# Transposing four token tiles on TensorE between query chunks, and loading eight tiles from SP's queue

## The chip, the cores and the metric

The kernel runs on one core of a Trainium2 chip. The metric is the device time of one execution in microseconds (us). The engines are named as in the profile: PE (TensorE: matmuls, with its weight loads as PEld), DVE (VectorE), ACT (ScalarE), POOL (GpSimd) and SP (SyncE, which here only issues DMAs). Each engine works through its own instructions in order. DMAs are issued in order by the engine in whose program they stand; they then share the core's 16 DMA engines.

## The reference

`x` has 2048 tokens of 512 values. It is normalised, and the result `xn` goes two ways: attention `A` with 32 heads of 128 against given keys and values (2048 each), and a mixer with an MLP, `B`, whose `silu` gates the attention's output.

```
xn = layernorm(x)                                    # 2048 x 512
A:  q = xn @ wq  (32 heads x 128);  p = softmax(q k^T / sqrt(128));  s = (p v) @ wo
B:  h = gelu(layernorm(xn) @ w1);  four column groups of h shifted by +1, -1, +2, -2 tokens
    x1 = xn + shifted(h) @ w2;  b = x1 + gelu(layernorm(x1) @ w3) @ w4      # F = 1792
out = x + s * silu(b)
```

Inputs and output are bf16.

## The kernel before

Tokens are worked in 16 tiles of 128 (`t`), and in four groups of 512 columns (`qt`). `xall[:, t, :]` holds normalised tile `t` with tokens on the partitions. Matmuls that contract over the 512 features need it transposed: `xnT`, four blocks of 128 features with all tokens as columns. The second layer norm of `B` is of an already normalised tile, so `m1` takes `xnT` as it is.

The order on every engine is written out by hand: each instruction is pinned in program order. The work up to the attention goes as follows.

- `load_x(t, eng)` (L153) loads a tile into `xin`, one of ten buffers of tag `ta`. Tiles 0 to 3 are loaded from SP and ACT, 4 to 7 from SP, 8 to 15 from GpSimd.
- `ln1_stats(t)` takes mean and variance on DVE (L172, L173) and the inverse root on POOL (`rsqrt`, L167, L168); `ln1_norm(t)` writes `xall` on DVE (L177) and frees `xin`.
- `tr_pe(t)` transposes a tile by four matmuls against the identity into one of the two PSUM buffers of `psO` and copies it to `xnT` on ACT (L191); `tr_dma(t)` does it with one transposing DMA on SP's queue (L194). Before, tiles 0 to 3 take the first way, all others the second.
- `m1(c0, w)` is the first product of `B` (PE, and gelu on ACT, L205); `m2(t)` the second, from the shifted columns, into `psO`; `x1(t, ps)` adds it to `xall` on DVE (L217).
- `q_ahead(u)` is one query chunk: four matmuls of 512 columns into a `psX` buffer, and a copy to `qT` on ACT (L269). Sixteen of them, one head and one `qt` each, are made ahead of the attention. Chunks 0 to 3 need `xnT` of tiles 0 to 3 alone.
- The seven loads of `w3` (L423) and that of `w2` (L384) stand on SP's queue; `ln2(t)` transposes the second normalised tiles by DMA on the same queue (L225); `m3` and `m4` are the MLP.

A DMA on SP or ACT also waits for the landing of the one eight DMAs earlier in their common program order, whose semaphore it takes over. All matmuls have line L106, a helper, so they are told apart by their tiles: `ps_q` is a query chunk, `ps_s<-xnT,w_sb` is `m1`, `ps_o<-w_sb,hT` is `m2`, and `ps_o<-ident,xall` is a transposition.

Behind this start lie the MLP (to about 129 us) and the attention with the output projection, in which scores, exponentials and the products with `v` run in slots (to the end). PE's order around the change is: transpositions and `m1` of tiles 0 to 3, query chunks 0 to 3, `m2(0)` and `m2(1)`, `m1(512, 512)` (tiles 4 to 7), chunks 4 to 7, `m2(2)` and `m2(3)`, `m1(1024, 512)` (tiles 8 to 11), and so on.

Of the kernel before, what the change touches and what calls it, by code (L numbers as in the profile page):

```python
# [17 lines left out]
def kernel(  # L18
# [15 lines left out]
    nc = tc.nc  # L34
    P = nc.NUM_PARTITIONS
# [12 lines left out]
    FC = F // P  # L48
    EPS = 1e-5
    SCALE = float(Dh) ** -0.5  # L50
    HG = 4
# [10 lines left out]
    pin = tc.keep_in_program_order  # L62
# [40 lines left out]
    w3_v = B_w3.rearrange("(dc p) f -> p dc f", p=P)  # L103

    def mm(out, lhsT, rhs, start, stop):
        pin(nc.tensor.matmul(out=out, lhsT=lhsT, rhs=rhs, start=start, stop=stop))  # L106
# [7 lines left out]
        out=ident[:], in0=diag[:], scalar1=0.0, scalar2=None, op0=ALU.is_equal))  # L114
# [36 lines left out]
    def load_x(t, eng):  # L151
        xin[t] = tokp.tile([P, D], BF16, tag="ta", bufs=10, name="xin")
        pin(eng.dma_start(out=xin[t][:], in_=xsrc[t]))  # L153
# [5 lines left out]
    w3_sb = [pL.tile([P, DC, 2 * P], BF16, name=f"w3_sb{i}") for i in range(FC // 2)]  # L159
# [21 lines left out]
    def ln1_stats(t):  # L181
        stats(xin[t][:], mv1, rs1, t)

    def ln1_norm(t):
        norm_to(xall[:, t, :], xin.pop(t)[:], mv1, rs1, t)

    def tr_pe(t):
        tp = psO.tile([P, DC, P], FP32, tag="ps_o", name="ps_o")
        for dc in range(DC):
            mm(tp[:, dc, :], xall[:, t, dc * P:(dc + 1) * P], ident[:], True, True)  # L190
        pin(nc.scalar.activation(out=xnT[:, :, t * P:(t + 1) * P], in_=tp[:], func=ACT.Identity))  # L191

    def tr_dma(t):
        pin(nc.sync.dma_start_transpose(out=xnT[:, :, t * P:(t + 1) * P], in_=xall[:, t, :]))  # L194

    def m1(c0, w):
        for jp in range(DC // 2):
            b = BASE_J[2 * jp]
            ps = psS.tile([P, 2, 512], FP32, name="ps_s")
            for j in range(2):  # L200
                jc = 2 * jp + j
                for dc in range(DC):
                    mm(ps[:, j, 0:w], w1_sb[:, dc, jc * P:(jc + 1) * P],
                       xnT[:, dc, c0:c0 + w], dc == 0, dc == DC - 1)
            pin(nc.scalar.activation(  # L205
                out=hT[:, 2 * jp:2 * jp + 2, b + c0:b + c0 + w], in_=ps[:, :, 0:w],
                func=ACT.Gelu_apprx_tanh))

    def m2(t):
        ps = psO.tile([P, D], FP32, tag="ps_o", name="ps_o")  # L210
        for jc in range(DC):
            c0 = BASE_J[jc] + t * P - SHIFT[jc]
            mm(ps[:], hT[:, jc, c0:c0 + P], w2_sb[:, jc, :], jc == 0, jc == DC - 1)
        return ps
# [41 lines left out]
    def q_mm(u, dcs, tag="xa"):  # L256
        g, qt, hh = units[u]
        if dcs[0] == 0:
            st[u] = dict(psq=psX.tile([P, 512], FP32, tag=tag, name="ps_q"))
        for dc in dcs:  # L260
            mm(st[u]["psq"][:], wqs[g * HG + hh][:, dc, :],
               xnT[:, dc, qt * 512:(qt + 1) * 512], dc == 0, dc == DC - 1)

    def q_copy(u, eng=None):
        qT = qtp.tile([P, 512], BF16, name="qT")
        if eng is None:
            pin(nc.vector.tensor_copy(out=qT[:], in_=st[u].pop("psq")[:]))  # L267
        else:
            pin(nc.scalar.activation(out=qT[:], in_=st[u].pop("psq")[:], func=ACT.Identity))  # L269
        st[u]["qT"] = qT  # L270
# [133 lines left out]
    ln1_norm(3)  # L404
    tr_pe(3)
    m1(256, 256)
    for t in range(8, 12):
        load_x(t, nc.gpsimd)

    def ln1_block(ts):  # L410
        ln1_stats(ts[0])
        for a, b in zip(ts, ts[1:]):
            ln1_stats(b)
            ln1_norm(a)
            tr_dma(a)
        ln1_norm(ts[-1])
        tr_dma(ts[-1])

    ln1_block(range(4, 8))
    for t in range(12, 16):  # L420
        load_x(t, nc.gpsimd)
    for i in range(FC // 2):
        pin(nc.sync.dma_start(out=w3_sb[i][:], in_=w3_v[:, :, i * 2 * P:(i + 1) * 2 * P]))  # L423
    def q_ahead(u):
        q_mm(u, range(DC), ("xa", "xm")[u % 2])
        q_copy(u, nc.scalar)

    for u in range(HG):
        q_ahead(u)
    pend = [(t, m2(t)) for t in range(2)]  # L430
    ln1_block(range(8, 12))
    m1(512, 512)
    for t, ps in pend:
        x1(t, ps)
    for u in range(HG, 2 * HG):
        q_ahead(u)
    pend = [(t, m2(t)) for t in range(2, 4)]
    ln1_block(range(12, 16))
    m1(1024, 512)
    for t, ps in pend:  # L440
        x1(t, ps)
# [92 lines left out]
    for n in range(NS + 3 * SPU):  # L534
        u, p = divmod(n, SPU)
# [25 lines left out]
        if p == 6 and wo_todo:  # L561
            gg, t = wo_todo.popleft()
# [13 lines left out]
    while wo_todo:  # L576
        gg, t = wo_todo.popleft()
# [36 lines left out]
```

## Time and profile before

| what | value |
|---|---|
| median of 3 runs | 1289.25 us (1289.19 to 1290.49) |
| profiled execution | 1289.44 us, span 1287.6 us |
| mean granted clock of TensorE | 0.991 |
| PE busy | 1257.4 us, 98% of the span |
| ACT busy | 1054.8 us, 82% |
| DVE busy | 942.5 us, 73% |
| POOL busy | 47.5 us, 4% |
| DMA | 91.57 MB, mean 71 GB/s |

The span runs from the first to the last instruction of the core; the time of the execution holds the little that lies around it. A row of instructions gives their start, their duration, the engine, the line, the operation, what is written from what, and their count; in brackets stands how long the engine was idle before and what ended that wait. A matmul's duration holds its way through the array, so matmuls in a row overlap, and what each costs is read from the distance of starts. "Granted clock" is the share of full speed that PE's clock was allowed; `PEclk` 1.00 is full.

### The profile page before, as it was taken

What the parts mean: (1) busy time and instruction counts of PE and PEld (TensorE: products, weight loads), DVE (VectorE), ACT (ScalarE), POOL (GpSimd) and SP (SyncE); (2) the same over time, 40 slices, a digit from 0 to 9 for tenths busy, and PEclk for the clock granted to TensorE, in tenths of its full rate; (3) what the DMA queues carried; (4) which work ended last, traced back from release to release, by engine and by line L of the source; (5) the groups of instructions that cost most, each with busy time, mean ns of one, the idle gap of its engine ahead of it and who ended that gap; (6) DMA issues with size and microseconds to landing.
All of it is one profiled execution on the core that took longest, in us unless ns stands there. A gap on an engine that the chain in (4) does not pass through costs nothing.

```text
span 1287.6 us, 16764 instructions
## 1 busy us (share of the span) xinstructions
PE 1257.4 (98%) x6128; PEld 609.6 (47%) x6252; DVE 942.5 (73%) x1316; ACT 1054.8 (82%) x1101; POOL 47.5 (4%) x115
## 2 busy tenths in 40 slices
PE   7999999999999999999999999999999999999995
PEld 3444444444444444444444444444444444444442
DVE  6721467777777777777777777777777777778886
ACT  4344779998888888888888888888888888888882
POOL 5320000000000000000000000000000000000000
PEclk9999999999999999999999999999999999999997
DMA  9293122443144522452145423451244323442211
GB/s 209 45 172 74 21 46 50 82 91 67 41 74 77 97 34 51 90 96 46 48 83 77 79 42 59 90 95 33 55 91 78 62 51 72 85 82 43 65 43 49
DMA packets 170771, 91.57 MB, mean 71 GB/s; under 512 B 124928, under 2 KB 153088, under 8 KB 170688
## 3 DMA queue, kind: packets, MB, share of 16 engines
q1 hardware_dynamic: 166464, 84.72, 34.3%
q0 software_dynamic: 1824, 4.98, 1.7%
q8 instruction: 49, 0.80, 0.3%
q10 hardware_dynamic: 2400, 0.79, 0.2%
q14 instruction: 34, 0.28, 0.1%
HBM read 67.63 MB, written 2.36 MB: 54 GB/s over the span
## 4 chain that ended last, share of the span: by engine, by line
PE 89%; DVE 6%; DMA 2%; ACT 1%; issue 1%; POOL 0%; another core or an unknown queue 0%; SPq 0%; DVEq 0%; ACTq 0%
PE ps_s L106 36%; PE ps_o L106 35%; PE ps_wo L106 8%; PE ps_q L106 7%; DVE acc L294 2%; PE ps_m L106 2%; PE ps_sum L106 1%; ACT pT L283 1%; DVE sacc L365 1%; DVE xall L369 1%; DVE acc L299 1%; DMA kT<-in_A_k_cache_dram 1%; DVE qT L267 0%; DVE xl L371 0%; DMA xnT<-xall 0%
## 5 line engine op out<-in xcount | busy, mean ns | idle before, releaser
L283 ACT ACTIVATE pT<-ps_s 128x1024 bf16<-128x1024 f32 x1024 | 993.1, 1026 | 135.3 <-PE ps_s L106 130.4
L106 PE MATMUL ps_o<-pT,vb 128*128 128x512 bf16 x2030 | 605.0, 379 | 3.3
L106 PE MATMUL ps_s<-qT,kT 128*128 128x512 bf16 x1986 | 596.8, 380 | 3.9 <-ACT pT L283 1.2
L294 DVE TENSOR_TENSOR acc<-acc,pT 128x2048 bf16<-128x2048 bf16 x256 | 312.3, 1220 | 72.3 <-ACT pT L283 71.2
L106 PEld LDWEIGHTS <-kT 128*128 128x128 bf16 x2048 | 222.0, 113 | 203.0 <-issue 6.1
L106 PEld LDWEIGHTS <-vb 128*128 128x128 bf16 x2048 | 199.9, 98 | 225.7
L289 DVE TENSOR_TENSOR acc<-pT 128x2048 bf16<-128x2048 bf16 x128 | 156.8, 1225 | 51.2 <-ACT pT L283 51.2
L106 PE MATMUL ps_wo<-wo_h,oT 128*128 128x512 bf16 x509 | 154.5, 387 | 6.2 <-DVE sacc L365 3.1
L365 DVE TENSOR_TENSOR sacc<-ps_wo,sacc 128x512 f32<-128x512 f32 x112 | 77.4, 691 | 89.5 <-PE ps_wo L106 88.7
L106 PE MATMUL ps_q<-xnT,wq_h 128*128 128x512 bf16 x481 | 141.6, 379 | 0.2
L299 DVE TENSOR_TENSOR acc<-acc 128x1024 bf16<-128x1024 bf16 x128 | 88.5, 691 | 4.4
L333 DVE TENSOR_TENSOR oT<-ps_o,rb 128x512 bf16<-128x512 f32 x128 | 87.3, 682 | 2.6 <-DMA rb<-dr 2.6
L106 PEld LDWEIGHTS <-oT 128*128 128x128 bf16 x512 | 50.4, 99 | 70.2 <-issue 7.6
L106 PEld LDWEIGHTS <-wq_h 128*128 128x128 bf16 x512 | 50.0, 98 | 60.4 <-issue 0.3
L267 DVE CAST qT<-ps_q 128x512 bf16<-128x512 f32 x112 | 76.3, 682 | 0.0
L300 DVE TENSOR_TENSOR acc<-acc 128x512 bf16<-128x512 bf16 x128 | 54.4, 425 | 4.4
L106 PEld LDWEIGHTS <-acc 128*128 128x128 bf16 x512 | 37.6, 116 | 34.2 <-issue 4.0
L355 POOL DMA_DIRECT2D xl<-in_A_x_dram x16 | 8.7, 543 | 1137.4 <-DMA out_dram<-xl 1014.3
L106 PE MATMUL ps_s<-xn2T,w_sb 128*128 128x512 bf16 x220 | 48.6, 379 | 0.2
L106 PEld LDWEIGHTS <-w_sb 128*128 128x128 bf16 x304 | 30.0, 99 | 39.1 <-issue 7.7
L234 ACT ACTIVATE h2T<-ps_s 128x1024 bf16<-128x1024 f32 x28 | 28.7, 1024 | 24.0 <-PE ps_s L106 23.3
L319 DVE RECIPROCAL rc<-ps_sum 128x4 f32<-128x4 f32 x128 | 23.2, 181 | 21.3 <-PE ps_sum L106 7.2
(45 smaller groups left out, 332.2 us busy)
## 6 DMA issues: line engine op xcount, KB each, us to landing
rb<-dr SPq DMA_DIRECT2D x128, 256.0 KB, 4.3
vb<-in_A_v_cache_dram SPq DMA_DIRECT2D x64, 256.0 KB, 4.4
wo_h<-in_A_wo_dram SPq DMA_DIRECT2D x32, 128.0 KB, 4.2
wq_h<-in_A_wq_dram SPq DMA_DIRECT2D x28, 128.0 KB, 4.5
w_sb<-in_B_w_dram SPq DMA_DIRECT2D x9, 256.0 KB, 5.4
kT<-in_A_k_cache_dram SPq DMA_TRANSPOSE x128, 4.4
xl<-in_A_x_dram POOLq DMA_DIRECT2D x16, 128.0 KB, 2.3
dr<-rc SPq DMA_DIRECT2D x128, 2.0 KB, 1.4
```

What stands on the lines that cost most here:

```text
L106: pin(nc.tensor.matmul(out=out, lhsT=lhsT, rhs=rhs, start=start, stop=stop))
L234: pin(nc.scalar.activation(out=h2[c, f][:], in_=ps[:], func=ACT.Gelu_apprx_tanh))
L267: pin(nc.vector.tensor_copy(out=qT[:], in_=st[u].pop("psq")[:]))
L283: pin(nc.scalar.activation(out=s["pT"][-1][:, jj:jj + 2, :], in_=sps[:], func=ACT.Exp, scale=SCALE))
L289: pin(nc.vector.tensor_tensor(out=s["acc"][:], in0=s["pT"][0][:], in1=s["pT"][1][:], op=ALU.add))
L294: pin(nc.vector.tensor_tensor(out=a[:], in0=a[:], in1=st[u]["pT"][i][:], op=ALU.add))
L299: pin(nc.vector.tensor_tensor(out=a[:, 0:2, :], in0=a[:, 0:2, :], in1=a[:, 2:4, :], op=ALU.add))
L300: pin(nc.vector.tensor_tensor(out=a[:, 0, :], in0=a[:, 0, :], in1=a[:, 1, :], op=ALU.add))
L319: pin(nc.vector.reciprocal(out=rc[:], in_=ps[:]))
L333: pin(nc.vector.tensor_tensor(out=oTs[(g, qt)][:, hh, :], in0=s["o"][:], in1=s["rb"][:], op=ALU.mult))
L365: pin(nc.vector.tensor_tensor(out=sa, in0=ps[:], in1=sa, op=ALU.add))
L369: pin(nc.vector.scalar_tensor_tensor(out=gl, in0=sa, scalar=0.5, in1=gl, op0=ALU.mult, op1=ALU.mult))
```

## The change

`tr_q(t)` is new: it runs query chunk `t - 4` and then transposes tile `t` on PE. For tiles 4 to 7 it takes the place of `tr_dma(t)`, and the loop over chunks 0 to 3 goes. So PE's order becomes chunk 0, tile 4, chunk 1, tile 5, chunk 2, tile 6, chunk 3, tile 7, `m2(0)`, `m2(1)`, `m1(512, 512)`: 16 weight loads and 16 matmuls more on PE, four copies more on ACT, four DMA transpositions fewer on SP. The loads of tiles 8 to 15 move from GpSimd, where they stood in two blocks of four, to SP, in one block ahead of the normalisation of tiles 4 to 7 and so ahead of the `w3` loads.

```diff
-    for t in range(8, 12):
-        load_x(t, nc.gpsimd)
-
-    def ln1_block(ts):
+    def ln1_block(ts, tr):
         ln1_stats(ts[0])
         for a, b in zip(ts, ts[1:]):
             ln1_stats(b)
             ln1_norm(a)
-            tr_dma(a)
+            tr(a)
         ln1_norm(ts[-1])
-        tr_dma(ts[-1])
-
-    ln1_block(range(4, 8))
-    for t in range(12, 16):
-        load_x(t, nc.gpsimd)
-    for i in range(FC // 2):
-        pin(nc.sync.dma_start(out=w3_sb[i][:], in_=w3_v[:, :, i * 2 * P:(i + 1) * 2 * P]))
+        tr(ts[-1])
+
     def q_ahead(u):
         q_mm(u, range(DC), ("xa", "xm")[u % 2])
         q_copy(u, nc.scalar)
 
-    for u in range(HG):
-        q_ahead(u)
+    def tr_q(t):
+        q_ahead(t - 4)
+        tr_pe(t)
+
+    for t in range(8, 16):
+        load_x(t, nc.sync)
+    ln1_block(range(4, 8), tr_q)
+    for i in range(FC // 2):
+        pin(nc.sync.dma_start(out=w3_sb[i][:], in_=w3_v[:, :, i * 2 * P:(i + 1) * 2 * P]))
     pend = [(t, m2(t)) for t in range(2)]
-    ln1_block(range(8, 12))
+    ln1_block(range(8, 12), tr_dma)
...
-    ln1_block(range(12, 16))
+    ln1_block(range(12, 16), tr_dma)
```

## The prediction

> **What bounds the kernel now.** I read the page's busy shares and its chain first, then the busy time of each engine in stretches cut at the places of the change, then the time line of those places. The page:
>
> ```profile
> span 1287.6 us, 16764 instructions
> PE 1257.4 (98%) x6128; PEld 609.6 (47%) x6252; DVE 942.5 (73%) x1316; ACT 1054.8 (82%) x1101; POOL 47.5 (4%) x115
> PE 89%; DVE 6%; DMA 2%; ACT 1%; issue 1%; POOL 0%; another core or an unknown queue 0%; SPq 0%; DVEq 0%; ACTq 0%
> ```
>
> PE is busy nearly throughout, so time is won or lost only where PE stands still, runs slowly or gets other work. By stretches (start:end, length, busy time per engine, granted clock, DMA share, GB/s):
>
> ```profile
> 13.36:18.81 5.45, 5.40 (x26) 2.34 (x24) 3.52 (x11) 3.02 (x6) 4.83 (x11) 1.00 0.64 141
> 18.81:21.75 2.94, 0.00 (x0) 0.03 (x1) 2.59 (x7) 0.00 (x0) 2.03 (x6) 1.00 0.96 235
> 21.75:26.67 4.92, 4.92 (x15) 1.90 (x16) 4.16 (x9) 1.03 (x1) 2.03 (x5) 0.65 1.33 298
> 32.10:129.14 97.04, 96.57 (x440) 43.72 (x448) 37.83 (x78) 41.46 (x47) 21.30 (x48) 1.00 0.49 97
> 1268.67:1287.60 18.93, 7.74 (x17) 1.91 (x16) 9.73 (x16) 0.00 (x0) 0.00 (x0) 0.50 0.20 49
> ```
>
> Ahead of 32 us there is one empty stretch, 2.94 us long, and the stretch behind it has a granted clock of 0.65. From 32.10 to 129.14 PE is idle for 97.04 - 96.57 = 0.47 us, so what PE gains before 32 us is carried along whole, unless a transfer comes late. The chain in order of time names what the empty stretch waits for:
>
> ```profile
> 16.09 0.56 DVE bn L172
> 16.65 4.86 DMA xnT<-xall
> 21.51 0.24 issue
> 21.75 5.30 PE ps_s L106 x16
> ```
>
> It is the DMA transposition of tile 7: issued at 16.65, landed at 21.51, after which `m1(512, 512)` starts. The slow clock is seen in PE's stretches of 3.41 us (busy, granted clock, DMA share, GB/s):
>
> ```profile
> 5.74:9.16 3.42, 2.07 (x20) 1.00 1.13 284
> 19.39:22.81 3.42, 1.06 (x5) 1.00 0.99 256
> 22.81:26.22 3.41, 3.41 (x9) 0.50 1.21 294
> ```
>
> A stretch with 1.06 us of work is followed by one at half clock; one with 2.07 us is not. So the wait costs twice, as idle time and as half clock.
>
> [...]
>
> **Part 1: the DMA transpositions of tiles 4 to 7 and their wait go.** PE's time line:
>
> ```profile
> 7.07 0.40 PE L106 MATMUL ps_o<-ident,xall 128*128 128x128 bf16 x4 [0.67 <-DVE xall L177]
> 9.90 0.61 PE L106 MATMUL ps_o<-ident,xall 128*128 128x128 bf16 x8
> 11.72 1.91 PE L106 MATMUL ps_s<-xnT,w_sb 128*128 128x256 bf16 x16 [1.22 <-ACT xnT L191]
> 13.68 3.40 PE L106 MATMUL ps_q<-xnT,wq_h 128*128 128x512 bf16 x15
> 16.92 1.89 PE L106 MATMUL ps_o<-w_sb,hT 128*128 128x512 bf16 x8
> 21.75 5.30 PE L106 MATMUL ps_s<-xnT,w_sb 128*128 128x512 bf16 x16 [2.94 <-DMA xnT<-xall]
> 30.37 1.89 PE L106 MATMUL ps_o<-w_sb,hT 128*128 128x512 bf16 x8
> 32.10 3.62 PE L106 MATMUL ps_s<-xnT,w_sb 128*128 128x512 bf16 x16
> 39.04 3.70 PE L106 MATMUL ps_o<-w_sb,hT 128*128 128x512 bf16 x15
> ```
>
> The idle time is worth 2.94 us. The half clock: the block `m1(512)` plus four query chunks lasts from 21.75 to 30.37, 8.62 us; the same block at full clock lasts from 32.10 to 39.04, 6.94 us. The difference is 1.68 us. [...] I take 1.68, since in the new order no gap between 13.4 and 32 us exceeds a few tenths.
>
> **Part 2: 16 transposing matmuls on PE.** Each tile adds four weight loads and four matmuls of 128 columns. Four take 0.40 us, eight 0.61, so four more cost 0.21 to 0.22, some 0.055 each in a row. Sixteen: 0.88 us, on the path, as PE has no hole there. Upper bound: nothing overlaps, and each costs what one alone lasts:
>
> ```profile
> L106 PE MATMUL ps_o<-ident,xall 128*128 128x128 bf16 x16 | 1.4, 220 | 0.7 <-DVE xall L177 0.7
> ```
>
> 16 x 0.220 = 3.52 us. I take 0.88: the row of eight is the same operation at the same place.
>
> [...]
>
> Do the tiles come in time? The normalisations (L177) of tiles 4 to 7:
>
> ```profile
> 12.21 0.41 DVE L177 TENSOR_SCALAR xall<-xin,mv,rs 128x512 bf16<-128x512 bf16 x1 [1.24 <-POOL rs L168]
> 13.36 0.38 DVE L177 TENSOR_SCALAR xall<-xin,mv,rs 128x512 bf16<-128x512 bf16 x1
> 14.51 0.41 DVE L177 TENSOR_SCALAR xall<-xin,mv,rs 128x512 bf16<-128x512 bf16 x1
> 15.68 0.41 DVE L177 TENSOR_SCALAR xall<-xin,mv,rs 128x512 bf16<-128x512 bf16 x1 [0.77 <-POOL rs L168]
> ```
>
> They end at 12.62, 13.74, 14.92 and 16.09. A query chunk takes 4 x 0.216 = 0.86 us (sixteen matmuls from about 13.46, one record being missing, to 16.92). PE asks for tile 4 at 13.46 + 0.86 = 14.3 and for tile 7 at 13.46 + 4 x 0.86 + 3 x 0.22 = 17.6, each time 1.5 us or more after it is ready. Cost zero, and it stays zero if a normalisation slips by a microsecond.
>
> **Part 3: four more copies on ACT** (L191), alternating with the four query copies (L269):
>
> ```profile
> 10.59 1.08 ACT L191 ACTIVATE xnT<-ps_o 128x512 bf16<-128x512 f32 x2
> 14.53 0.60 ACT L269 ACTIVATE qT<-ps_q 128x512 bf16<-128x512 f32 x1 [0.27 <-PE ps_q L106]
> ```
>
> Two in a row take 1.08 us, so about 0.48 from start to start. Per chunk ACT has some 1.0 us of work, PE 0.86 + 0.22 = 1.08: PE leads. At the end ACT trails: the last query product is done at about 17.8, its copy at 18.4, tile 7's copy at 18.9 to 19.0. `m2(0)` fills 17.9 to 18.7; `m2(1)` needs tile 7's PSUM buffer (`psO` has two) and waits some 0.25 us. Bounds: 0, and the 1.22 us that `m1(256, 256)` waited for two such copies. I take 0.25, since `m2(0)` lies between here and nothing did there. `m1(512)` itself then finds tile 7 copied.
>
> **Part 4: queues.** POOL loses eight issues:
>
> ```profile
> 8.87 2.40 POOL L153 DMA_DIRECT2D xin<-in_A_x_dram  x4
> 15.60 2.23 POOL L153 DMA_DIRECT2D xin<-in_A_x_dram  x4
> ```
>
> Each block stands between sums of statistics and `rsqrt` (L167, L168), so the normalisations of tiles 4 to 11 can only come earlier, by up to 2.40 + 2.23 us. They are off PE's path; I book nothing. SP gains eight loads and loses four transpositions:
>
> ```profile
> 7.72 0.38 SPq L384 DMA_DIRECT2D w_sb<-in_B_w_dram  x1
> 12.65 5.23 SPq L194 DMA_TRANSPOSE xnT<-xall  x4
> 17.93 5.12 SPq L423 DMA_DIRECT2D w_sb<-in_B_w_dram  x7
> 23.15 11.59 SPq L194 DMA_TRANSPOSE xnT<-xall  x8
> ```
>
> The new loads issue in order behind `w2_sb` (7.72). Loads 10 to 15 reuse the `ta` buffers of tiles 0 to 5, so load 15 waits for tile 5's normalisation (13.74) and for the landing of `w2_sb`, whose semaphore it takes over. Behind it stand the seven `w3` loads and the transpositions of tiles 8 to 15. Landing times, one row each for `w2_sb` (issued 7.72) and the transposition of tile 11 (issued at 28.02):
>
> ```profile
> w_sb<-in_B_w_dram SPq DMA_DIRECT2D x1, 512.0 KB, 4.4
> xnT<-xall SPq DMA_TRANSPOSE x1, 3.8
> ```
>
> `w2_sb` lands at 12.1. So load 15 goes at 13.8 at the latest, `w3` at 14.2 to 19.3, and the transposition of tile 11 at 19.3 + 3 x 1.45 = 23.7 (eight in 11.59: 1.45 each), landing at 27.5. Its normalisation is no limit:
>
> ```profile
> 22.24 0.41 DVE L177 TENSOR_SCALAR xall<-xin,mv,rs 128x512 bf16<-128x512 bf16 x1 [0.77 <-POOL rs L168]
> ```
>
> It ended at 22.65 already. PE asks for tiles 8 to 11 at 32.10 less the gain. Before, tile 11 landed at 28.02 + 3.8 = 31.8, only 0.3 us ahead of PE: this cover is thin, and the gain exists only because SP runs about 4 us earlier too. That is the next thing to be late. Tiles 12 to 15 follow by another 4 x 1.45 us and are needed only behind the `m2` group that began at 39.04; everything later on SP, POOL and DVE is set off by PE's products and moves with them.
>
> **Sum.** 2.94 + 1.68 - 0.88 - 0.25 = 3.49 us; PE would ask for tile 11 at 32.10 - 3.49 = 28.6, 1.1 after it landed. The profiled execution took 1289.44 us (span 1287.6 plus 1.84), 0.19 above the median of 1289.25, so the sum gives 1289.44 - 3.49 = 1285.95; forecast 1286.0.
>
> **Rivals.**
> [...]
> - *Transpositions do not overlap with the query chunks' weight loads* and cost 0.220 each: 4.62 - 3.52 - 0.25 = 0.85: 1288.6. The row of eight speaks against it. [...]
> - *The wait moves whole to `m1(1024)`:* tiles 8 to 11 land as before at 31.8. PE idles from 28.6 to 31.8 and pays the half clock again: 3.49 - 3.2 - 1.68 = -1.4, so 1290.8, still within 0.2%.
> - *Slower: SP is blocked at load 15.* All of `w3` and the transpositions of tiles 8 to 15 stand behind it. If it goes only at 20 us rather than 13.8, tile 11 lands at 27.5 + 6.2 = 33.7; PE idles 5.1 us and pays 1.68: 3.49 - 6.8 = -3.3, so 1292.7. It is slower than before from the point where tile 11 lands after about 30.4 (28.6 + 3.49 - 1.68), and by over 0.2% from 33.0. Against it: every wait of load 15 ends by 13.8 in this trace. For it: 1 MB of loads and 1.75 MB of `w3` now stand in one queue ahead of the transpositions.
>
> **How the numbers follow.** A difference under 0.2% (2.6 us) can't be told from no change here. Forecast 0.60 (1285.0 to 1287.0, of which 0.02 lies within 0.2%); only the idle time 0.18; no overlap 0.06; wait moved 0.06; slower 0.10. Faster: 0.58 plus 0.02 of the second case, in which half the slow clock goes too, 0.60. Same: 0.02 + 0.16 + 0.06 + 0.06 = 0.30. Slower: 0.10. The range's lower end is the gain with both costs halved, 4.62 - 0.44 - 0.12 = 4.06, less 0.7 for where the gate falls at the end of the kernel (17 matmuls at half clock in the last stretch quoted): 1284.7. Its upper end takes in the second and third case with 0.9 us to spare for the same reason: 1289.5. Outside are the moved wait and the slower case, 0.16. The likeliest case alone: 1285.0 to 1287.0.
>
> **What would show it.** Right: no wait of PE for a transfer in front of `m1(512)`; that block starts near 19.9; granted clock 1.00 from 13 to 30 us; four L191 copies between the L269 ones; `m1(1024)` near 28.6 without a wait. Wrong: PE waits for `xnT` by DMA at `m1(1024)`, transposing groups longer than 0.3 us per tile, a wait of `m2(1)` for ACT near 1 us, or load 15 after 18 us.

## The result and the profile after

| | before | after |
|---|---|---|
| median, measured side by side | 1289.88 us (8 runs, 1289.19 to 1291.47) | 1285.80 us (8 runs, 1285.54 to 1285.91) |
| ratio, 95% interval | | 0.9966 [0.9957, 0.9975] |
| profiled execution, span | 1289.44 us, 1287.6 us | 1285.54 us, 1283.8 us |
| `m1(512, 512)` starts | 21.75 us | 19.64 us |
| `m1(1024, 512)` starts | 32.10 us | 28.31 us |

The changed kernel is 0.34% faster, 4.1 us between the medians and 3.9 between the profiled executions. Forecast were 1286.0 us and a range of 1284.7 to 1289.5.

The page of the changed kernel, the lines that answer to those of before:

```profile
span 1283.8 us, 16912 instructions
PE 1263.9 (98%) x6268; PEld 611.3 (48%) x6268; DVE 942.8 (73%) x1316; ACT 1056.8 (82%) x1105; POOL 43.1 (3%) x107
PE 92%; DVE 5%; ACT 1%; DMA 1%; issue 0%; POOL 0%; DVEq 0%; ACTq 0%
```

The chain has lost its transposing DMA; PE's share of it went from 89% to 92%. PE's busy time is no measure of the change: the profile of before lacks matmul records (6128 beside 6252 weight loads), the one after has all 6268. Busy time of the engines by stretches of the changed kernel (same columns as before, granted clock third from the end):

```profile
13.32:17.70 4.38, 4.38 (x35) 2.49 (x33) 3.34 (x9) 3.91 (x8) 2.49 (x6) 1.00 1.01 287
17.70:19.64 1.94, 1.88 (x11) 0.77 (x9) 1.68 (x6) 1.03 (x2) 1.24 (x4) 1.00 1.19 301
19.64:23.10 3.46, 3.46 (x18) 1.56 (x17) 2.85 (x6) 1.03 (x1) 0.82 (x3) 1.00 1.59 134
28.31:125.34 97.03, 97.03 (x449) 43.79 (x448) 37.92 (x78) 41.47 (x47) 21.46 (x48) 1.00 0.49 95
```

Chunks and transpositions fill 4.38 us without a gap, the clock stays at 1.00, and `m1(512)` takes 3.46 us where it took 4.92. From `m1(1024)` on PE is not seen idle at all (97.03 of 97.03 us). PE's time line of the changed kernel at the place of the change:

```profile
16.58 1.03 PE L106 MATMUL ps_q<-xnT,wq_h 128*128 128x512 bf16 x4
17.45 0.39 PE L106 MATMUL ps_o<-ident,xall 128*128 128x128 bf16 x4
17.70 2.11 PE L106 MATMUL ps_o<-w_sb,hT 128*128 128x512 bf16 x8
19.64 3.62 PE L106 MATMUL ps_s<-xnT,w_sb 128*128 128x512 bf16 x16
28.31 3.62 PE L106 MATMUL ps_s<-xnT,w_sb 128*128 128x512 bf16 x16
```

SP's queue in the changed kernel, and the landing of tile 11's transposition, issued at 22.68:

```profile
8.56 4.37 SPq L153 DMA_DIRECT2D xin<-in_A_x_dram  x8
12.98 4.34 SPq L428 DMA_DIRECT2D w_sb<-in_B_w_dram  x7
17.41 11.96 SPq L194 DMA_TRANSPOSE xnT<-xall  x8
```

```profile
xnT<-xall SPq DMA_TRANSPOSE x1, 2.6
```

Tile 11 lands at 22.68 + 2.6 = 25.3; it landed at 31.8 before. PE needs it at 28.3.

### The profile page after: what moved, and what is told of

Read it like the earlier page. It is cut to its first block, busy times and chain, and to the rows that moved or that the text cites. A ratio compares the mean times of both kernels' runs of the same rounds, so it can differ in the third digit from the quotient of the medians.

```text
span 1283.8 us, 16912 instructions
## 1 busy us (share of the span) xinstructions
PE 1263.9 (98%) x6268; PEld 611.3 (48%) x6268; DVE 942.8 (73%) x1316; ACT 1056.8 (82%) x1105; POOL 43.1 (3%) x107
## 4 chain that ended last, share of the span: by engine, by line
PE 92%; DVE 5%; ACT 1%; DMA 1%; issue 0%; POOL 0%; DVEq 0%; ACTq 0%
PE ps_s L106 37%; PE ps_o L106 35%; PE ps_wo L106 9%; PE ps_q L106 8%; DVE acc L294 2%; PE ps_m L106 2%; PE ps_sum L106 1%; DVE sacc L365 1%; DVE xall L369 1%; DVE acc L299 1%; DVE qT L267 0%; DVE xl L371 0%; DMA rb<-dr 0%; ACT pT L283 0%; ACT xnT L191 0%
## 5 line engine op out<-in xcount | busy, mean ns | idle before, releaser
L106 PE MATMUL ps_s<-qT,kT 128*128 128x512 bf16 x2048 | 609.7, 379 | 1.3 <-ACT pT L283 1.2
L106 PE MATMUL ps_q<-xnT,wq_h 128*128 128x512 bf16 x512 | 148.3, 379 | 0.0
L234 ACT ACTIVATE h2T<-ps_s 128x1024 bf16<-128x1024 f32 x28 | 28.7, 1024 | 24.0 <-PE ps_s L106 24.0
```

The lines of the kernel that those rows point to most:

```text
L234: pin(nc.scalar.activation(out=h2[c, f][:], in_=ps[:], func=ACT.Gelu_apprx_tanh))
```

## The experiments

Two theories stood at first. *Mine:* the hole in front of `m1(512)` and the half clock behind it are the price, and both go with the DMA transpositions. *The rival:* SP's and POOL's queues bring the gain. The fourth run showed that neither is enough; from then on the question was whether tile 11's landing is a second bound that lies right behind the hole. Each kernel's median is compared with runs of the kernel before on the same chip; those had medians of 1289.1 to 1289.3 us.

**Only the queues.**

```diff
-    for t in range(8, 12):
-        load_x(t, nc.gpsimd)
+    for t in range(8, 16):
+        load_x(t, nc.sync)
...
-    for t in range(12, 16):
-        load_x(t, nc.gpsimd)
```

> Tiles 4 to 7 stay with the DMA transpositions and chunks 0 to 3 stay in a row; only the loads of tiles 8 to 15 move to SP. My theory (the gain is the hole in front of m1(512, 512) and the half clock behind it): nothing gained, the transposition of tile 4 now stands behind load 15 on SP, so 1289 to 1291 us against 1289.9 before, with PE still waiting about 3 us for xnT and a stretch of 3.4 us at half clock. Rival (POOL's relief and the queue order bring the gain): 1286 to 1287 us.

1288.51 us, ratio 0.9998 [0.9988, 1.0007]: no gain that can be told. PE's waits up to 60 us in this kernel (us in total, times, longest):

```profile
PE ps_s L106 <- DMA xnT<-xall: 3.8, 2, 2.5
```

Its time line at the two waits:

```profile
20.15 3.61 PE L106 MATMUL ps_s<-xnT,w_sb 128*128 128x512 bf16 x16 [1.26 <-DMA xnT<-xall]
31.48 3.61 PE L106 MATMUL ps_s<-xnT,w_sb 128*128 128x512 bf16 x16 [2.50 <-DMA xnT<-xall]
```

In place of the one wait were two: 1.26 us at `m1(512)` and 2.50 at `m1(1024)`, which started at 31.48, with no half clock behind either (granted clock 1.00 from 12 to 36 us). So my "about 3 us and half clock at `m1(512)`" was wrong in its parts, while the time came out 0.5 us under my range, with nothing gained as I had said, for a reason that only the fourth run made plain.

**Only the transpositions.** The changed kernel with the loads of tiles 8 to 15 on GpSimd, in blocks ahead of and behind the normalisation of tiles 4 to 7.

```diff
-    for t in range(8, 16):
-        load_x(t, nc.sync)
+    for t in range(8, 12):
+        load_x(t, nc.gpsimd)
     ln1_block(range(4, 8), tr_q)
+    for t in range(12, 16):
+        load_x(t, nc.gpsimd)
```

> Only the transpositions of tiles 4 to 7 on PE between the query chunks; the loads of tiles 8 to 15 stay on GpSimd in two blocks. My theory: as the changed kernel, 1285.4 to 1286.2 us. The rival of the queues: 1288.5 us or more, with PE waiting at m1(1024, 512) for tiles 8 to 11.

1286.17 us, 0.9975 [0.9965, 0.9985]; `m1(1024)` at 28.32, as in the changed kernel. Moving the loads was not needed for the gain: SP, without four transpositions in front, issued `w3` from 8.30 on. Its queue, and the landing of tile 11:

```profile
8.30 5.95 SPq L430 DMA_DIRECT2D w_sb<-in_B_w_dram  x7
19.08 12.01 SPq L194 DMA_TRANSPOSE xnT<-xall  x8
```

```profile
xnT<-xall SPq DMA_TRANSPOSE x1, 3.1
```

Tile 11's transposition, issued at 23.98, landed 3.1 us later, at 27.1, 1.2 us before PE came to `m1(1024)`. So this kernel too has both: no hole, and SP's queue earlier at tile 11.

**No interleaving.**

```diff
     def tr_q(t):
-        q_ahead(t - 4)
+        if t == 4:
+            for u in range(HG):
+                q_ahead(u)
         tr_pe(t)
```

> As the changed kernel, but chunks 0 to 3 run first and tiles 4 to 7 are transposed behind them. My theory: tiles 6 and 7 and both m2 products wait in turn for PSUM buffers that ACT copies out at 0.5 us each; m1(512, 512) starts about 1.2 us later than in the changed kernel, full clock: 1286.7 to 1287.3 us. Rival (the interleaving is of no account): 1285.8 us.

1286.92 us, 0.9983 [0.9974, 0.9992]. PE's time line:

```profile
16.67 0.61 PE L106 MATMUL ps_o<-ident,xall 128*128 128x128 bf16 x8
18.01 0.87 PE L106 MATMUL ps_o<-ident,xall 128*128 128x128 bf16 x8 [0.73 <-ACT xnT L191]
19.07 1.89 PE L106 MATMUL ps_o<-w_sb,hT 128*128 128x512 bf16 x8 [0.19 <-ACT xnT L191]
20.80 3.62 PE L106 MATMUL ps_s<-xnT,w_sb 128*128 128x512 bf16 x16
```

`m1(512)` starts 1.16 us later than in the changed kernel, and the waits are for ACT's copies out of the two buffers: the chunks between the tiles hide them.

**The hole filled.** The kernel before, with PE kept busy where it waited.

```diff
     pend = [(t, m2(t)) for t in range(2)]
+    fill = psX.tile([P, 512], FP32, tag="xa", name="ps_fill")
+    for _ in range(13):
+        mm(fill[:], warm[:, 0:P], warm[:], True, True)
```

> The kernel before with 13 matmuls on zeroes (2.8 us at full clock, result unused) on PE behind m2(1), where it waited. My theory: the hole costs as before, but the clock stays up behind it, so 1.7 us are saved: 1287.9 to 1288.6 us against 1289.9. Rival (the half clock costs nothing of its own, only the idle time counts): 1289.9 us.

1288.94 us, 0.9997 [0.9988, 1.0006] against a kernel before at 1289.26: no saving that can be told, and the interval ends at 1.5 us saved, short of my 1.7. That is as the rival said, but not for the rival's reason. The clock did stay up, and `m1(512)` took 3.45 us:

```profile
18.44 2.97 PE L106 MATMUL ps_fill<-warm 128*128 128x512 bf16 x13
21.25 3.62 PE L106 MATMUL ps_s<-xnT,w_sb 128*128 128x512 bf16 x16
24.70 3.65 PE L106 MATMUL ps_q<-xnT,wq_h 128*128 128x512 bf16 x16
28.19 1.89 PE L106 MATMUL ps_o<-w_sb,hT 128*128 128x512 bf16 x8
31.84 1.46 PE L106 MATMUL ps_s<-xnT,w_sb 128*128 128x512 bf16 x6 [1.77 <-DMA xnT<-xall]
```

PE then waited 1.77 us at `m1(1024)`, which began at 31.84 as against 32.10. The chain in order of time of this kernel:

```profile
28.34 3.37 DMA xnT<-xall
31.84 3.62 PE ps_s L106 x16
```

Tile 11 landed at 31.7. The half clock had only filled the time until then.

**SP's queue as before, PE's order as after.** The kernel of "only the transpositions", plus the four DMAs into a tile that nobody reads (lines move by one).

```diff
     def tr_q(t):
         q_ahead(t - 4)
         tr_pe(t)
+        pin(nc.sync.dma_start_transpose(out=scr[:, :, (t - 4) * P:(t - 3) * P], in_=xall[:, t, :]))
```

> The changed PE order, but SP's queue as before: tiles 4 to 7 are transposed on PE and, beside that, by the four DMAs on SP into a scratch tile that nobody reads; the loads of tiles 8 to 15 stay on GpSimd, so w3 and the transpositions of tiles 8 to 15 issue as late as before. My theory after the run with the filled hole (tile 11's landing near 31.8 us is a second bound right behind the hole): PE comes to m1(1024, 512) at 28.3 and waits some 3.3 us there, with up to 1.7 us of half clock: 1289.1 to 1290.8 us. Rival (the hole in front of m1(512, 512) alone was the price): 1285.8 to 1286.3 us.

1290.69 us, 1.0013 [1.0003, 1.0022]: slower than before, though PE has no hole in front of `m1(512)`. Its time line, and the stretch at half clock behind the wait (columns as in the views by stretches above):

```profile
19.74 3.62 PE L107 MATMUL ps_s<-xnT,w_sb 128*128 128x512 bf16 x16
23.19 3.65 PE L107 MATMUL ps_q<-xnT,wq_h 128*128 128x512 bf16 x16
26.68 1.89 PE L107 MATMUL ps_o<-w_sb,hT 128*128 128x512 bf16 x8
31.83 3.70 PE L107 MATMUL ps_s<-xnT,w_sb 128*128 128x512 bf16 x10 [3.26 <-DMA xnT<-xall]
```

```profile
32.60:36.01 3.41, 3.41 (x10) 1.21 (x8) 1.25 (x4) 1.03 (x1) 2.19 (x6) 0.50 0.39 78
```

The wait moved whole, 3.26 us, and took the half clock along. This is the mechanism of the prediction's rival "the wait moves whole to `m1(1024)`": 1290.8 forecast there, 1290.69 measured. The four DMAs are all that sets this kernel apart from "only the transpositions" at 1286.17: with them tile 11's transposition is issued at 28.08 rather than 23.98.

**The kernel before once more.** No edit.

> The kernel before, profiled once more, to see how its two waits and its half clock differ from one execution to the next. Theory of two bounds: PE's start of m1(1024, 512) stays at 31.5 to 33 us however the hole in front of m1(512, 512) and the clock fall. Rival (hole and half clock add up freely): that start moves by the size of the half clock, to about 30.5 in an execution without it.

1289.07 us. PE's time line, with its waits in brackets:

```profile
21.16 3.61 PE L106 MATMUL ps_s<-xnT,w_sb 128*128 128x512 bf16 x16 [2.33 <-DMA xnT<-xall]
24.61 3.65 PE L106 MATMUL ps_q<-xnT,wq_h 128*128 128x512 bf16 x15
28.10 1.89 PE L106 MATMUL ps_o<-w_sb,hT 128*128 128x512 bf16 x8
31.69 3.61 PE L106 MATMUL ps_s<-xnT,w_sb 128*128 128x512 bf16 x16 [1.71 <-DMA xnT<-xall]
```

In this execution the clock stayed full (1.00 from 12 to 36 us), the hole was 2.33 us, and yet `m1(1024)` began at 31.69: a second wait, 1.71 us, stands where the first profile had the half clock. The kernel is the same.

**`w3` later.** The kernel before, with the seven `w3` loads behind the transpositions of tiles 12 to 15; then the same with the 13 filling matmuls.

```diff
-    for i in range(FC // 2):
-        pin(nc.sync.dma_start(out=w3_sb[i][:], in_=w3_v[:, :, i * 2 * P:(i + 1) * 2 * P]))
...
     ln1_block(range(12, 16))
+    for i in range(FC // 2):
+        pin(nc.sync.dma_start(out=w3_sb[i][:], in_=w3_v[:, :, i * 2 * P:(i + 1) * 2 * P]))
     m1(1024, 512)
```

> The kernel before with the seven w3 loads moved behind the transpositions of tiles 12 to 15 on SP; nothing else. Theory of two bounds: tile 11 lands some 4 us earlier and tile 7, no longer beside the w3 traffic, up to 2 us earlier; the hole in front of m1(512, 512) shrinks to 1 to 2 us, none is left at m1(1024, 512): 1285.8 to 1287.5 us. Rival (SP's backlog is of no account, only where tiles 4 to 7 are transposed): 1289.3 us.

1287.56 us, 0.9989 [0.9980, 0.9999], just above my range. The second wait is gone; the first is not smaller than in the last run:

```profile
21.09 3.61 PE L106 MATMUL ps_s<-xnT,w_sb 128*128 128x512 bf16 x16 [2.31 <-DMA xnT<-xall]
24.54 3.65 PE L106 MATMUL ps_q<-xnT,wq_h 128*128 128x512 bf16 x15
28.03 1.89 PE L106 MATMUL ps_o<-w_sb,hT 128*128 128x512 bf16 x8
29.75 3.62 PE L106 MATMUL ps_s<-xnT,w_sb 128*128 128x512 bf16 x16
```

I had expected tile 7 to land sooner without `w3` beside it. It took 4.18 us from its issue at 16.64, where the first profile of before has 4.86 and the second about 4.5 (an estimate from SP's row, 12.37 for the first of the four issues, and the start of `m1(512)` at 21.16); `w3` was at most a small part of what delayed it.

> The same with the hole filled by 13 matmuls on zeroes (2.8 us). With w3 out of the way the second bound is gone, so the filling now sets the time: m1(512, 512) starts near 21.3, full clock, no wait at m1(1024, 512): 1287.4 to 1287.9 us; against 1288.9 for the filled hole with w3 in its old place. Rival (no second bound): 1288.9 us as there.

1287.05 us, 0.9987 [0.9977, 0.9996]; the profiled execution took 1287.33. That is a little under my range. `m1(512)` starts at 21.40 and `m1(1024)` at 30.07, both without a wait. With the hole filled and `w3` in its old place it was 1288.94: taking the second bound away gains 1.9 us, and the time follows PE again. What the filling itself gains here isn't shown: the intervals of the two kernels overlap, and the profiled execution of the unfilled one had no half clock to save (1.00 from 12 to 36 us).

**The price of a transposition on PE.**

```diff
-        for dc in range(DC):
+        for dc in [d for _ in range(2 if t >= 4 else 1) for d in range(DC)]:
             mm(tp[:, dc, :], xall[:, t, dc * P:(dc + 1) * P], ident[:], True, True)
```

> The changed kernel with the four transposing matmuls of each of tiles 4 to 7 issued twice: 16 more. My theory (0.055 us each, in a row): 1286.7 us, between 1286.5 and 1287.0. Rival (0.220 us each): 1289.3 us.

1286.36 us, 0.9977 [0.9967, 0.9986], a little under my lower bound. Eight in a row take 0.44 us from start to start (14.10 to 14.54), so 0.055 each:

```profile
14.10 0.61 PE L106 MATMUL ps_o<-ident,xall 128*128 128x128 bf16 x8
14.54 1.03 PE L106 MATMUL ps_q<-xnT,wq_h 128*128 128x512 bf16 x4
```

From the first chunk to `m1(512)` PE takes 20.23 - 13.23 = 7.00 us, where the changed kernel takes 19.64 - 13.32 = 6.32: 0.68 more rather than 0.88, because the wait of `m2(1)` for ACT is gone.

**The tile ahead of its chunk.**

```diff
-        q_ahead(t - 4)
         tr_pe(t)
+        q_ahead(t - 4)
```

> The changed kernel with each tile's transposition ahead of its query chunk, so that ACT ends with a query copy and m2(1) no longer waits for tile 7's copy. My theory: 0.2 us less, 1285.6 us (1285.4 to 1285.8), the wait of m2(1) gone. Rival (the normalisations are late by then and PE waits for DVE): 1286 us or more.

1285.45 us, 0.9973 [0.9963, 0.9984]. From the first tile to `m1(512)` 19.70 - 13.62 = 6.08 us, 0.24 less than in the changed kernel; the wait of `m2(1)` is gone. The medians of the two were taken apart, so the 0.35 us between them is no measurement; the 0.24 are the time line's.

**Tiles 8 to 11 on PE too.**

```diff
-    ln1_block(range(8, 12), tr_dma)
+    ln1_block(range(8, 12), lambda t: None)
...
     for u in range(HG, 2 * HG):
         q_ahead(u)
+        tr_pe(u + 4)
```

> The changed kernel with tiles 8 to 11 transposed on PE as well, one behind each of chunks 4 to 7, in place of their DMAs. My theory (PE has no hole there, the transpositions only add): 0.9 to 1.2 us more, 1286.7 to 1287.0. Rival (a transposition on PE is a gain as such): 1285.8 us or less.

1286.75 us, 0.9982 [0.9972, 0.9992]. From `m1(512)` to `m1(1024)` it takes 29.50 - 19.72 = 9.78 us, 8.67 in the changed kernel: 1.11 more, the price of sixteen transpositions and the wait of `m2(3)`, with no hole to set against it.

**DMA transpositions in time.** The kernel before, with the queue in another order.

```diff
-    for t in range(8, 12):
-        load_x(t, nc.gpsimd)
+    for t in range(8, 14):
+        load_x(t, nc.sync)
...
     ln1_block(range(4, 8))
-    for t in range(12, 16):
-        load_x(t, nc.gpsimd)
+    for t in range(14, 16):
+        load_x(t, nc.sync)
```

and `w3` behind tile 15, as above.

> The DMA transpositions of tiles 4 to 7 kept, the loads of tiles 8 to 13 moved to SP ahead of them and 14 and 15 behind them (so none of them waits for a buffer in front of a transposition), w3 behind tile 15. POOL is relieved as in the changed kernel. Theory: tile 7 is normalised by 14.9, its DMA issues by 15.5 and lands by 18 to 19, about when PE is there (18.5): no hole over 0.5 us, no transposition on PE: 1284.6 to 1285.3 us. Rival (DMA transpositions cannot be in time for m1(512, 512)): 1286 us or more.

1284.59 us, 0.9965 [0.9951, 0.9979], at the lower edge of my range. The median is 1.2 us under that of the changed kernel, but the two were not measured side by side, and their ratios to the kernel before (0.9965 and 0.9966) are the same. What can be read is the time lines: `m1(1024)` starts at 27.31 here and at 28.31 in the changed kernel. PE's time line and tile 7's landing, issued at 15.64:

```profile
16.92 1.89 PE L106 MATMUL ps_o<-w_sb,hT 128*128 128x512 bf16 x8
18.64 3.62 PE L106 MATMUL ps_s<-xnT,w_sb 128*128 128x512 bf16 x16
27.31 3.62 PE L106 MATMUL ps_s<-xnT,w_sb 128*128 128x512 bf16 x16
```

```profile
xnT<-xall SPq DMA_TRANSPOSE x1, 2.4
```

Tile 7 is there at 18.0, PE at 18.64: no hole, and no transposition on PE. The hole of before was a matter of when the DMAs went, not of DMA as such.

**All runs in one line.** The start of `m1(1024)` and the time of the profiled execution:

| kernel | `m1(1024)` starts | time | difference |
|---|---|---|---|
| before | 32.10 | 1289.44 | 1257.34 |
| before again | 31.69 | 1289.07 | 1257.38 |
| only the queues | 31.48 | 1288.59 | 1257.11 |
| hole filled | 31.84 | 1288.96 | 1257.12 |
| SP's queue as before | 31.83 | 1290.73 | 1258.90 |
| `w3` later, hole filled | 30.07 | 1287.33 | 1257.26 |
| `w3` later | 29.75 | 1287.30 | 1257.55 |
| tiles 8 to 11 on PE | 29.50 | 1286.80 | 1257.30 |
| no interleaving | 29.47 | 1286.82 | 1257.35 |
| transposed twice | 28.89 | 1286.04 | 1257.15 |
| tile first | 28.36 | 1285.28 | 1256.92 |
| only the transpositions | 28.32 | 1286.18 | 1257.86 |
| after | 28.31 | 1285.54 | 1257.23 |
| DMA in time | 27.31 | 1284.54 | 1257.23 |

With the exception of the kernel whose half clock lies behind that start, the difference is 1257.4 within 0.5 us. (There the half clock, with nothing left behind it to wait for, cost 1258.9 - 1257.4 = 1.5 us, by one profile.) So the time of this kernel is decided by when `m1(1024)` can start, which is the later of two things: PE's way there, and tile 11's landing.

## Why the prediction was right, and where its sum was not

- *Idle time, 2.94 us, and half clock, 1.68 us:* on PE both went as said: no wait at `m1(512)`, clock 1.00, and the block from `m1(512)` to `m2(2)` takes 26.58 - 19.64 = 6.94 us, 1.68 less than before. But neither is a price that is saved by itself, as "the wait costs twice" has it, and as the case "only the idle time" takes for granted with 2.94 - 0.88 - 0.25 = 1.81 us. In the kernel before tile 11 landed at 31.8, 0.3 us ahead of PE, so PE without the half clock would have waited there: it did in the second profile of before (1.71 us) and with the hole filled (1.77 us). Without hole and half clock alike it waited 3.26 us (SP's queue as before). What made PE's gain count was SP's queue, 6.5 us earlier at tile 11. The prediction said so under the queues ("the gain exists only because SP runs about 4 us earlier too") but did not carry it into that case's 1.81 us: the second profile of before had no half clock, and yet `m1(1024)` began 31.69 - 28.31 = 3.38 us later there than in the changed kernel. That the 1.68 fits is luck in part: the start of `m1(1024)` was near 32 by either bound, with the half clock (32.10) or without it (31.69).
- *Where the half clock falls:* the 0.18 for only the idle time, and the range's margins for the end of the kernel, 0.7 us at its lower end and 0.9 at its upper, were my estimates of this; no run shows these terms. What the runs showed is a granted clock of 0.50 from 1270 to 1283 us in the profiles of before and after alike, and, in the table above, 0.94 us between the shortest and the longest time behind the start of `m1(1024)` (1256.92 to 1257.86), without the one kernel whose half clock lies there.
- *Sixteen transpositions, 0.88 us:* chunks and tiles together took 4.38 us against 3.46 for the chunks, 0.92. The doubled run gives 0.055 us each. The rival of 0.220 each does not hold for these matmuls in a row against an identity.
- *ACT's copies, 0.25 us:* 0.21, the 1.94 us of `m2(0)` and `m2(1)` less the 1.73 that eight such matmuls take from 26.58 to 28.31. The kernel with the tile ahead of its chunk takes it away.
- *Queues:* that the cover at tile 11 was thin, and that the gain rests on SP running earlier, was said and is shown by the kernels with and without the four extra DMAs (1290.69 and 1286.17). Load 15 was no obstacle: the eight loads were issued by 12.93, expected by 14.2 at the latest. Tile 11 landed at 25.3 rather than 27.5. Of this 1.0 us is its issue, at 22.68 rather than 23.7: tile 5 was normalised by 12.57, not 13.74, since POOL issued no loads ahead of it, and load 15 went sooner. The other 1.2 us is its way, 2.6 rather than 3.8; that the way would be shorter was not foreseen.
- *What is left of the gain:* 32.10 - 28.31 = 3.79 us, where the sum had 3.49. Of the rest 0.14 is that the profiled execution after reached the place earlier from its first microseconds on (`m1(256, 256)` at 11.58 instead of 11.72). The other 0.16 is that the hole, read from starts, was 21.75 - 16.92 - 1.73 = 3.10 us: the idle time of 2.94 begins only at the end of the 1.89 us that the row of `m2` counts as busy. The median of before was also 0.4 us over its profiled execution in that comparison.

## What to carry to other kernels

Where an engine waits, look at the next wait of the same kind and at its margin: a hole filled or a slow stretch sped up is worth only the distance to the next bound, and here, with 0.3 us of margin, 1.7 us of half clock were worth no more than that by themselves. When a transfer is moved off a queue, what stands behind it in the queue may gain more than what it fed: with only the transpositions moved, tile 11 landed at 27.1 rather than 31.8, while `m1(512)` started at 19.65 rather than 21.75. Before replacing a late DMA by work on the engine that is the bound, try to issue it earlier: here that brought `m1(1024)` another 1.0 us forward, with no work added to PE.

## What the runs showed that was not expected

- *Not every hole brings a half clock.* Holes of 2.94 and 3.26 us were followed by 3.41 us at clock 0.50; holes of 2.33 (the same kernel as the first), 2.31 and 2.50 us were not (1.00). So the profile of one execution can show a half clock that another execution of the same kernel lacks. Whether the length of the hole or its position decides is not shown; no run varied the position by itself.
- *The same DMA transposition landed after 2.4 us or after 4 to 5.* Tile 7's landed 2.4 us after its issue in "DMA in time" and in "only the queues" (17.47 to 19.90), while the DMA engines were busy at a share of 0.43 (15 to 18 us) and 0.47 (18 to 21 us). It took 4.2 to 4.9 us in the kernels that load tiles 12 to 15 from GpSimd just then (`w3` later, at a share of 0.79 from 18 to 21 us; before, 0.98 over the 4.86 us). `w3` later without much effect, and "only the queues" with `w3` still right behind tile 7 but those loads gone ahead, point at these loads; moving them alone was not tried.
- *The kernel before varies more than the one after:* 1289.19 to 1291.47 against 1285.54 to 1285.91, eight runs each, side by side. The two kernels with `w3` later spread as well (1286.5 to 1288.8, 1287.0 to 1288.7). Why is not shown; none of the longer executions was profiled.
